# An mLSTM cell followed by a gated feed-forward block: three loads and one join of the first cells at other places in their queues

## The chip, the core and the metric

The kernel runs on one core of a Trainium2 chip. A core has a matrix engine (TensorE, PE in the profile, with its weight loads shown apart as PEld), a vector engine (VectorE, DVE), a scalar engine for activation functions (ScalarE, ACT), a general engine (GpSimd, POOL), and a queue processor (SyncE, SP) that here issues nearly all DMA transfers. Each engine takes its own instructions strictly in the order in which the program lists them, and they wait for one another through semaphores. The metric is the time of one execution on the device in microseconds (us), lower being better.

## The reference

The first half is a recurrent attention cell over 4 batches, 8 heads, 768 steps and a head width of 40; the second half multiplies its 3072 x 320 result by w_in (320 x 2048), applies h cos(h) and multiplies by w_out (2048 x 320).

```python
for t in range(S):
    m_new = np.maximum(f_gate[:, :, t] + m, i_gate[:, :, t])
    f_stab = np.exp(f_gate[:, :, t] + m - m_new)
    i_stab = np.exp(i_gate[:, :, t] - m_new)
    m = m_new
    C = f_stab[..., None, None] * C + i_stab[..., None, None] * np.einsum('bhd,bhe->bhde', vt, kt)
    n = f_stab[..., None] * n + i_stab[..., None] * kt
    h_tilde = np.einsum('bhde,bhe->bhd', C, qt)
    denom = np.maximum(np.abs(np.einsum('bhd,bhd->bh', n, qt)), 1.0)[..., None]
    y[:, :, t] = h_tilde / denom / (1.0 + np.exp(-o_gate[:, :, t]))
...
h = x @ w_in
return (h * np.cos(h)) @ w_out
```

## The kernel before

The recurrence is worked in chunks of 128 steps: 6 chunks c times 4 batches b make 24 cells, numbered n = 4c + b. In a cell, the scores q k^T of all 8 heads (`scores`, L440) are weighted by a decay matrix E and multiplied by v (`values`, L466); the state left by earlier chunks is added for n of 4 and more (`values_kept`). The result is normalized on VectorE (`normalize`), transposed on TensorE (`seam`) and copied by ScalarE into x^T (`seam_out`, L594), the input of the feed-forward block. That block works on one chunk of 512 tokens at a time. `Up` (L607) computes two 128-row blocks of h for a chunk: for each block one matmul with the first 128 rows of w_in, one with the second 128 (L621) and one with the last 64, held apart in `w_in_l` (L624). The profile shows every matmul of 32-bit floats as two instructions, so that an `Up` has four L621, four L621 again and four L624 there. `near`, `rest`, `sin` and `gate` turn h into h cos(h) on ScalarE and VectorE by turns; `down` multiplies by w_out (L754 in the first chunk, L697 later).

The program orders everything by hand. `first_cells` (L768) lists what happens for cells 0 to 3, before any feed-forward work; after it, `both_parts` (L904) runs one cell of chunk c + 1 beside two `Up`s of chunk c. Every call in `first_cells` adds its instructions to the ends of the queues of the engines it uses, so moving a call moves its instructions against all others on those engines, and on no other engine.

The steps that the change touches:

- `load(n, which)` (L315) issues the transfers of q, k and v of cell n on SP, 160 KB each, in rows of 40 numbers (L329). q, k and v have four buffers each, so cell 4 uses those of cell 0.
- `load_E(n)` (L340) issues, on SP, the broadcast of M, the running maximum of the gates, to all 128 partitions: 512 KB (L345). It lands in the tile E of the cell.
- `load_o` (L300) fetches o_gate, 160 KB a batch; `weights_in(f)` (L156) issues ten transfers that make three pieces of w_in: two with 128 rows each (four transfers each) and the last 64 rows (two transfers); `weights_out(p)` (L167) issues one of 640 KB. All these are on SP.
- The weights come as 64-bit floats, and are joined into 32-bit ones: `parts` (L132) works on ScalarE (L138, L140), and `join` (L143) runs three operations on VectorE (L144, L146, L148) and an addition (L149), on GpSimd unless VectorE is named.
- `decay_exponents(n)` (L370) subtracts a column from E on VectorE (L372) and masks it on GpSimd (L373); `decay(n)` takes Exp on ScalarE (L381). `weigh(n)` (L450) multiplies E by the scores (L453).

Up(0,0), the first feed-forward work, is special: between its first and second four matmuls it calls `cell_after_first` (L879):

```python
turn(B)                      # q and k of cell 4 transposed on TensorE
turn_out(B, False)           # copied by ScalarE
first_out = out_parts()      # w_out's first piece, L138 and L140 on ScalarE
decay(B)                     # Exp of cell 4 on ScalarE
weigh_k(B)
out_join(*first_out)         # w_out's first piece, L144 to L148 on VectorE
```

(B is 4.) After it, TensorE has the second four L621, the four L624 that use w_in_l, scores(4), values_kept(4), six warming matmuls and values(4).

Of the kernel before, what the change touches and what calls it, by code (L numbers as in the profile page):

```python
# [29 lines left out]
def kernel(  # L30
# [22 lines left out]
    B, H, S, D = q.shape  # L53
# [78 lines left out]
    def parts(dst, bits):  # L132
        n = dst.shape[1]
        hi, lo = bits[:, 0:n, 1], bits[:, 0:n, 0].bitcast(U32)
        t = p2.tile([128, WQ], I32, name="wt", tag="wt")[:, 0:n]
        m = p2.tile([128, WQ], I32, name="wm", tag="wm")[:, 0:n]

        nc.scalar.activation(out=t.bitcast(FP), in_=hi.bitcast(FP), func=AF.Abs)  # L138

        nc.scalar.activation(out=m, in_=lo, func=AF.Copy, scale=2.0 ** -29)  # L140
        return dst, hi, t, m

    def join(dst, hi, t, m, last=None):  # L143
        nc.vector.tensor_scalar(out=t.bitcast(FP), in0=t.bitcast(FP), scalar1=LEAST, scalar2=GREATEST,  # L144
                                op0=OP.max, op1=OP.min)
        nc.vector.tensor_scalar(out=t, in0=t, scalar1=5, scalar2=2, op0=OP.logical_shift_left,  # L146
                                op1=OP.logical_shift_right)
        nc.vector.scalar_tensor_tensor(out=t, in0=hi, scalar=TOP2, in1=t, op0=OP.bitwise_and, op1=OP.bitwise_or)  # L148
        (last or nc.gpsimd).tensor_tensor(out=dst.bitcast(I32), in0=t, in1=m, op=OP.add)  # L149
# [17 lines left out]
    def weights_out(p):  # L167
        bits = pc.tile([128, 2, DM, 2], I32, name="bits", tag="bits")
        src = w_out_bits.rearrange("(g e a r) n two -> g a r e n two", e=2, a=2, r=128)
        nc.sync.dma_start(out=bits, in_=src[p // 2, p % 2])  # L170
        return w_out_sb[:, ts(p, 2)].rearrange("p f n -> p (f n)"), bits.rearrange("p e n two -> p (e n) two")
# [29 lines left out]
    def later_fills():  # L201
        for i in range(1, NB):
            fill(i)
        for t in st:
            nc.gpsimd.memset(t, 0.0)
        for t in qbs:
            nc.gpsimd.memset(t[:, H * 64:], 0.0)
# [3 lines left out]
    def gates_in():  # L211
        nc.sync.dma_start(out=F0, in_=fg[:, 0:C])
        nc.scalar.dma_start(out=a0, in_=ig[:, 0:C])

    def later_gates_in():
        nc.sync.dma_start(out=F1.rearrange("r c s -> r (c s)"), in_=fg[:, C:])
        nc.sync.dma_start(out=a1.rearrange("r c s -> r (c s)"), in_=ig[:, C:])
# [74 lines left out]
    def load_o(c, bs=range(B)):  # L292
        if c not in sig:
            sig[c] = p2.tile([128, B * DM + LO], FP, name="o", tag="o")
            if c > 1:
                nc.gpsimd.memset(sig[c][:, B * DM:], 0.0)
        for b in bs:
            o = sig[c][:, ts(b, DM)]
            if c * B < TURNED:
                nc.sync.dma_start(out=o.rearrange("t (h d) -> t h d", h=H),  # L300
                                  in_=o_gate[b, :, ts(c, C)].rearrange("h t d -> t h d"))
                continue

            for k4 in range(HP):
                nc.sync.dma_start(out=o[ts(k4, 32)].rearrange("r (i x) -> r i x", i=2),
                                  in_=o_gate[b, ts(k4, 2), ts(c, C)].rearrange("i (r x) d -> r i (x d)", x=T4))
# [5 lines left out]
    def blocks(n):  # L312
        return [qbs[n % 2 + i].rearrange("r (p x) -> r p x", p=HP) for i in (0, 2)]

    def load(n, which="qkv"):  # L315
        c, b = divmod(n, B)
        i = n % NB
        if n >= TURNED:
            for dst, src in zip(blocks(n), (q, k)):
                src = src[b, :, ts(c, C)].rearrange("(p j) (r x) d -> j r p (x d)", j=2, x=T4)  # L320
                for j in range(2):
                    r = slice(64 * j, 64 * j + 32)
                    nc.sync.dma_start(out=dst[r], in_=src[j])
                    r = slice(64 * j + 32, 64 * j + 64)
                    nc.sync.dma_start(out=dst[r, :, 0:(T4 - 1) * D + DL], in_=src[j, :, :, DA:])
            which = "kv"
        for name, dst, src in (("q", qs[i], q), ("k", ks[i], k), ("v", vs[i], v)):
            if name in which:
                nc.sync.dma_start(out=dst[:, :, 0:D], in_=src[b, :, ts(c, C)].rearrange("h t d -> t h d"))  # L329
# [10 lines left out]
    def load_E(n):  # L340
        c, b = divmod(n, B)
        E = p4.tile([128, H, C], FP, name="E", tag="E")
        if n not in SPREAD:
            src = M_d[0][ts(b, H)] if c == 0 else M_d[1][ts(b, H), ts(c - 1, C)]
            nc.sync.dma_start(out=E, in_=src.unsqueeze(0).to_broadcast([128, H, C]))  # L345
        Es[n] = E
# [18 lines left out]
    def cols(n, j, width):  # L365
        c, b = divmod(n, B)
        return tab[:, c, j, ts(b, H)].unsqueeze(2).to_broadcast([128, H, width])


    def decay_exponents(n):  # L370
        E = Es[n]
        nc.vector.tensor_tensor(out=E, in0=E, in1=cols(n, 0, C), op=OP.subtract)  # L372
        nc.gpsimd.affine_select(out=E, in_=E, compare_op=OP.is_ge, fill=1.0e30, base=0,  # L373
                                pattern=[[0, H], [1, C]], channel_multiplier=-1)
# [388 lines left out]
    def warm(k, bank=None):  # L763

        for _ in range(k):
            nc.tensor.matmul(bank or pw, nil, nil.unsqueeze(1).to_broadcast([128, HP, 128]), start=True, stop=True)

    def first_cells():  # L768
        nc.vector.memset(nil, 0.0)
        gates_in()  # L770
        nc.scalar.copy(out=ident_b, in_=ident)
        load(0, "qk")
        later_gates_in()
        load(1, "qk")
        load(0, "v")
        load_o(0, (0, 1))
        load(2, "qk")
        load_E(0)
        load_E(1)
        warm(9)  # L780
        gates_first()
        later_fills()
        gates_first_out()
        wall_in(0, 0, pmu)
        wall_in(0, 1, psum_o())
        spread(0, 0)
        decay_exponents_half(0, 0)
        turn(0)
        turn_out(0, False)
        gates_sums()  # L790
        spread(0, 1)
        decay_exponents_half(0, 1)
        decay(0)
        weigh_k(0)
        load_E(2)
        load(1, "v")
        load(3, "qk")
        load_o(0, (2, 3))
        load_E(3)
        load(2, "v")  # L800
        load(3, "v")
        pieces.extend(weights_in(0))
        wall_in(1, 0, psum_o())
        wall_in(1, 1, psum_o())
        gates_less_sums()
        spread(1, 0)
        decay_exponents_half(1, 0)
        scores(0)
        gates_maxima()
        turn(1)  # L810
        weigh(0)
        turn_out(1, False)
        sigmoid(0, slice(0, 2))
        spread(1, 1)
        decay_exponents_half(1, 1)
        gates_exponents()
        decay(1)
        weigh_k(1)
        values(0)
        normalize(0)  # L820
        scores(1)
        turn(2)
        turn_out(2, False)
        warm(2)
        seam(0)
        weigh(1)
        seam_out(0)
        state(0)
        load(B)
        decay_exponents(2)  # L830
        decay(2)
        weigh_k(2)
        gates_exp()
        values(1)
        load_E(B)
        outs.append((0, weights_out(0)))
        load_o(1, (0,))
        load_E(B + 1)
        normalize(1)
        scores(2)  # L840
        turn(3)
        sigmoid(0, slice(2, 4))
        seam(1)
        weigh(2)
        decay_exponents(3)
        turn_out(3)
        gates_diagonal()
        seam_out(1)
        values(2)
        decay(3)  # L850
        weigh_k(3)
        state(1)
        normalize(2)
        scores(3)
        pg = gates_turn()
        warm(1)
        seam(2)
        weigh(3)
        join(*parts(*pieces.pop(0)))
        pieces.extend(weights_in(1))  # L860
        load(B + 1)
        outs.extend((p, weights_out(p)) for p in range(1, 3))
        load_o(1, (1, 2, 3))
        seam_out(2)
        second = parts(*pieces.pop(0))
        state(2)
        gates_keep(*pg)
        values(3)
        normalize(3)
        warm(5)  # L870
        seam(3)
        join(*second, nc.vector)
        decay_exponents(B)
        seam_out(3)
        join(*parts(*pieces.pop(0)), nc.vector)
        load_E(B + 2)
        state(3)

# [180 lines left out]
```

## Time and profile before

| | us |
|---|---|
| median of three runs | 540.45 |
| the three runs | 536.65, 540.67, 540.45 |
| the profiled execution's own time | 537.82 |
| its span in the profile | 536.1 |

The granted TensorE clock of the profiled execution is 1.0 throughout. The profile has the busy time of each engine, the waits with what released them, the chain of waits that ended last, and the order of instructions in time. Of the engine names, SPq, ACTq and DVEq mean the queue of an engine, in which it issues a transfer or passes a semaphore. A transfer's row on SPq is the time that issuing it took in the queue, what it waited for included; it lands later. Busy time of TensorE in a few stretches, from the view by windows:

| stretch, us | PE busy | DVE busy | ACT busy | DMA share | GB/s |
|---|---|---|---|---|---|
| 0 to 10 | 8.88 | 5.41 | 4.10 | 0.99 | 129 |
| 10 to 20 | 9.84 | 8.26 | 7.37 | 1.12 | 186 |
| 20 to 30 | 8.24 | 8.58 | 9.67 | 0.84 | 218 |
| 30 to 40 | 8.04 | 6.32 | 5.46 | 0.97 | 221 |
| 40 to 50 | 7.64 | 9.27 | 8.43 | 1.10 | 211 |
| 50 to 60 | 9.68 | 7.13 | 8.30 | 1.02 | 293 |
| 60 to 70 | 10.00 | 7.34 | 7.41 | 1.07 | 205 |

`first_cells` ends at about 35 us, where up(0,0) begins (L621 at 35.26).

### The profile page before, as it was taken

To read this page: it belongs to the slowest core of one execution; us is meant where nothing else is said; L and a number is where in the kernel's file an instruction comes from. 1 tells how busy PE (TensorE), PEld (TensorE's weight loads), DVE (VectorE), ACT (ScalarE), POOL (GpSimd) and SP (SyncE) were. 2 spreads that over 40 slices of the span, in tenths; PEclk is the share of its full clock that TensorE was granted. 3 is DMA by queue.
4 is the path that set the end of the run, shared out by engine and by line. 5 is a ranking of instruction groups with operands and counts; after the bars stand their busy time and mean duration, and the time that the engine had idled before them with its cause. 6 is when DMAs were issued, how large, how long until landed. Compare 5 with 4: busy or idle time off the path is not lost.

```text
span 536.1 us, 9942 instructions
## 1 busy us (share of the span) xinstructions
PE 524.8 (98%) x3634; PEld 332.6 (62%) x3634; DVE 365.7 (68%) x727; ACT 261.6 (49%) x416; POOL 168.0 (31%) x304
## 2 busy tenths in 40 slices
PE   9888999999999999999999999999999999999997
PEld 6755666665565666666666656656656756656555
DVE  6778778868677677777767777767776765422323
ACT  4868696765633445543436525427335322332312
POOL 7512433516253453223322322422212221212121
PEclk9999999999999999999999999999999999999999
DMA  9989995952265752166743076635075000010001
GB/s 139 214 214 250 230 225 164 196 113 46 73 139 125 165 109 62 51 140 144 159 99 82 14 174 134 141 82 123 6 177 107 14 15 11 6 49 0 2 0 49
DMA packets 134513, 56.86 MB, mean 106 GB/s; under 512 B 72081, under 2 KB 130529, under 8 KB 134465
## 3 DMA queue, kind: packets, MB, share of 16 engines
q1 hardware_dynamic: 134320, 56.04, 47.1%
q8 instruction: 28, 0.46, 0.4%
q0 software_dynamic: 96, 0.18, 0.2%
q14 instruction: 21, 0.16, 0.1%
q10 hardware_dynamic: 48, 0.02, 0.0%
HBM read 50.00 MB, written 6.21 MB: 105 GB/s over the span
## 4 chain that ended last, share of the span: by engine, by line
PE 80%; SPq 6%; DMA 5%; DVE 4%; ACT 4%; issue 1%; POOL 1%; DVEq 0%; ACTq 0%; POOLq 0%
PE po L697 32%; PE pup L621 28%; PE pup L624 9%; PE hp L490 3%; PE ps L447 3%; PE po L754 3%; DMA E<-M_d 2%; SPq L329 2%; PE hp L484 2%; SPq L129 1%; PE pu L586 1%; DMA bits<-in_moe_w_in_dram 1%; SPq L300 1%; DMA qs<-in_q_dram 1%; DVE n L632 1%
## 5 line engine op out<-in xcount | busy, mean ns | idle before, releaser
L621 PE MATMUL pup<-xT,w_in_sb 128*128 128x512 f32 x384 | 175.0, 598 | 0.7 <-DVE g L641 0.3
L629 ACT ACTIVATE n<-pup 128x512 int32<-128x512 f32 x96 | 52.0, 593 | 211.7 <-PE pup L624 211.7
L632 DVE SCALAR_TENSOR_TENSOR n<-pup,n 128x512 f32<-128x512 f32 x96 | 61.9, 686 | 122.1 <-ACT n L629 122.1
L697 PE MATMUL po<-w_out_sb,g 128*128 128x320 f32 (+1 forms) x480 | 118.6, 396 | 0.0
L621 PEld LDWEIGHTS pup<-xT,w_in_sb 128*128 128x128 f32 x384 | 69.7, 190 | 72.8 <-issue 63.4
L697 PEld LDWEIGHTS po<-w_out_sb,g 128*128 128x128 f32 x480 | 83.5, 190 | 36.7 <-issue 9.1
L680 POOL TENSOR_TENSOR sg<-g 128x128 f32<-128x128 f32 x80 | 36.7, 458 | 192.4 <-DVE g L641 191.0
L637 ACT ACTIVATE n<-n 128x512 f32<-128x512 f32 x96 | 58.9, 630 | 12.1 <-DVE n L632 12.1
L641 DVE SCALAR_TENSOR_TENSOR g<-pup,n 128x512 f32<-128x512 f32 x96 | 61.7, 685 | 2.5 <-ACT n L637 1.2
L624 PE MATMUL pup<-xT,w_in_l 64*128 64x512 f32 x192 | 54.2, 641 | 2.2 <-DVE w_in_l L149 2.2
L373 POOL TENSOR_SCALAR_AFFINE_SELECT E<-E 128x1024 f32<-128x1024 f32 x19 | 20.8, 1093 | 102.0 <-DVE E L372 81.0
L697 PE MATMUL po<-T,sg 128*128 128x160 f32 x240 | 39.4, 300 | 0.0
L624 PEld LDWEIGHTS pup<-xT,w_in_l 64*128 64x128 f32 x192 | 14.4, 184 | 38.7 <-issue 35.6
L754 PE MATMUL po<-w_out_sb,g 128*128 128x320 f32 x128 | 36.6, 439 | 0.1
L697 PEld LDWEIGHTS po<-T,sg 128*128 128x128 f32 x240 | 34.8, 190 | 0.2
L412 DVE STREAM_TRANSPOSE t<-qs 128x512 f32<-128x512 f32 x32 | 32.7, 1101 | 0.0
L447 PEld LDWEIGHTS ps<-t,t 40*128 40x128 f32 (+1 forms) x384 | 25.1, 188 | 9.7 <-issue 9.4
L453 DVE TENSOR_TENSOR E<-ps,E 128x512 f32<-128x512 f32 x48 | 30.7, 681 | 0.4 <-PE ps L447 0.4
L381 ACT ACTIVATE E<-E 128x1024 f32<-128x1024 f32 x21 | 22.2, 1057 | 17.4 <-POOL E L373 16.2
L754 PEld LDWEIGHTS po<-w_out_sb,g 128*128 128x128 f32 x128 | 23.7, 190 | 9.7 <-POOL w_out_sb L149 0.3
L447 PE MATMUL ps<-t,t 40*128 40x128 f32 (+1 forms) x384 | 25.8, 274 | 0.0
L372 DVE TENSOR_TENSOR E<-E,tab 128x1024 f32<-128x1024 f32 x19 | 23.1, 1216 | 3.3 <-DMA E<-M_d 3.3
(152 smaller groups left out, 640.6 us busy)
## 6 DMA issues: line engine op xcount, KB each, us to landing
E<-M_d SPq DMA_DIRECT2D x22, 512.0 KB
bits<-in_moe_w_in_dram SPq DMA_DIRECT2D x40, 128.0 KB
bits<-in_moe_w_out_dram SPq DMA_DIRECT2D x8, 640.0 KB
room<-G_d SPq DMA_DIRECT2D x32, 128.0 KB
ks<-in_k_dram SPq DMA_DIRECT2D x24, 160.0 KB
vs<-in_v_dram SPq DMA_DIRECT2D x24, 160.0 KB
qs<-in_q_dram SPq DMA_DIRECT2D x32, 80.0 KB
qs<-in_k_dram SPq DMA_DIRECT2D x32, 80.0 KB
```

The lines of the kernel that those rows point to most:

```text
L412: nc.vector.transpose(out=dst.rearrange("r p (t x) -> r p x t", x=T4), in_=src.rearrange("r p (x d) -> r p x d", x=T4)[:, :, :, 0:32])
L447: nc.tensor.matmul(ps[j][:, p], kT[r, p], qT[r, p], start=True, stop=True)
L453: nc.vector.tensor_tensor(out=w, in0=pss[n][j], in1=w, op=OP.mult)
L621: nc.tensor.matmul(pu, w_in_sb[:, i, ts(block(f2, e), 128)], x(i), start=(i == 0), stop=False)
L624: nc.tensor.matmul(pu, w_in_l[r, f2], x(NK, r), start=False, stop=True)
L629: nc.scalar.activation(out=self.n[e], in_=self.pu[e], func=AF.Copy, bias=0.25)
L632: nc.vector.scalar_tensor_tensor(out=self.n[e].bitcast(FP), in0=self.pu[e], scalar=0.25, in1=self.n[e], op0=OP.add, op1=OP.subtract)
L637: nc.scalar.activation(out=r, in_=r, func=AF.Sin, scale=TWO_PI_DOWN)
L641: nc.vector.scalar_tensor_tensor(out=g, in0=self.pu[e], scalar=TWO_PI, in1=self.n[e].bitcast(FP), op0=OP.mult, op1=OP.mult)
L680: nc.gpsimd.tensor_tensor(out=S[:, i], in0=x, in1=y, op=op)
L697: nc.tensor.matmul(out, g, w, start=(f2 == 0 and first), stop=end, skip_group_check=True)
L754: nc.tensor.matmul(po[c][b], gs[c, f][:, ts(b, C)], w_out_sb[:, f], start=(f == 0), stop=(f == NF - 1))
```

## The change

Five lines of `first_cells` move; no operation is added or taken away.

```diff
         load(3, "qk")
+        load(2, "v")
         load_o(0, (2, 3))
         load_E(3)
-        load(2, "v")
         load(3, "v")
         pieces.extend(weights_in(0))
...
         state(0)
-        load(B)
+        load_E(B)
+        load(B, "qk")
         decay_exponents(2)
...
         values(1)
-        load_E(B)
         outs.append((0, weights_out(0)))
+        load(B, "v")
         load_o(1, (0,))
...
         join(*second, nc.vector)
-        decay_exponents(B)
         seam_out(3)
         join(*parts(*pieces.pop(0)), nc.vector)
+        decay_exponents(B)
         load_E(B + 2)
```

On SP, v of cell 2 goes ahead of two loads of o_gate and of M of cell 3. M of cell 4 goes ahead of q, k and v of cell 4, and v of cell 4 goes behind w_out's first piece; the order there was q, k, v, M, w_out and is M, q, k, w_out, v. On VectorE, the four operations of the join of w_in's last 64 rows (L144, L146, L148 and L149, all on VectorE here) stand ahead of L372 of cell 4 instead of behind it. The order on TensorE, ScalarE and GpSimd is the same in both programs.

## The prediction, made before the changed kernel was run

> **What bounds the kernel now.** I read the page's busy table first, then who waited for whom on TensorE before and after 48 us, then the chain of waits between 26 and 49 us, then the order of time on each engine there.
>
> ```profile
> span 536.1 us, 9942 instructions
> PE 524.8 (98%) x3634; PEld 332.6 (62%) x3634; DVE 365.7 (68%) x727; ACT 261.6 (49%) x416; POOL 168.0 (31%) x304
> ```
>
> TensorE is busy 98% of the span, so only its holes can be won. From 48 us on, the view of waits for TensorE holds two entries, 0.5 us together. Before 48 us it holds these four among six:
>
> ```profile
> PE pup L624 <- DVE w_in_l L149: 2.2, 1, 2.2
> PE ph L472 <- DMA vs<-in_v_dram: 1.8, 1, 1.8
> PE pw L766 <- ACT st L600: 1.5, 1, 1.5
> PE pup L621 <- ACT xT L594: 0.2, 1, 0.2
> ```
>
> The change aims at the first (w_in's last rows, joined late on VectorE) and the second (v of cell 2). The chain of waits tells which of them carries the end (columns: start, us, what):
>
> ```profile
> 26.37 4.80 DMA bits<-in_moe_w_in_dram
> ...
> 31.27 0.67 ACT wt L138
> ...
> 32.26 5.68 DMA E<-M_d
> ...
> 38.03 1.23 DVE E L372
> ...
> 39.49 1.08 DVE wt L146
> ...
> 41.57 0.44 DVE w_in_l L149
> ...
> 42.05 1.13 PE pup L624 x4
> ...
> 44.17 1.29 DVE E L453 x2
> ```
>
> VectorE stands 2.52 us for M of cell 4 (E), subtracts, and only then joins w_in_l, for which TensorE stands 2.24 us. The v wait at 24.32 is not in it. The order of time on three engines gives the rows that I use (start, us, engine):
>
> ```profile
> 37.92 1.88 PE L621 MATMUL pup<-xT,w_in_sb 128*128 128x512 f32 x4
> 39.49 1.07 DVE L146 TENSOR_SCALAR wt<-wt 128x256 int32<-128x256 int32 x1
> 39.78 0.79 ACT L138 ACTIVATE wt<-bits 128x640 f32<-128x640 f32 x1 [1.02 <-DMA bits<-in_moe_w_out_dram]
> 41.13 1.04 ACT L381 ACTIVATE E<-E 128x1024 f32<-128x1024 f32 x1
> ```
>
> **The join ahead of the exponents.** VectorE is free at 35.50 (34.81 + 0.69), and ScalarE's two halves of that piece end at 35.76. The four operations without company cost 0.29 + 0.29 + 0.43 + 0.43 us (the same shapes at 39.17, 60.85, 61.18 and 41.57), with gaps 1.6 us: w_in_l is done at about 37.2 instead of 42.00. TensorE's second four L621 end at 39.80, so L624 starts there, not at 42.05: 2.25 us. Scores(4) start 0.96 us after it, and weigh(4) 1.16 us after those (43.01 and 44.17 now): 40.76 and 41.92.
>
> In place of that wait, three things could be late. First E4: its subtraction now starts after 37.2. M of cell 4 is issued where q of cell 4 was (28.36, with 1.40 us in the queue), and 5.68 us (now 32.26 to 37.94) puts it at 34.0 to 35.4, so the subtraction (1.23) ends at 38.4 and GpSimd's mask (1.09) at 39.6. Second, w_out's first piece stands on ScalarE ahead of cell 4's Exp: it lands at 39.7 now, 6.6 us after its issue at 33.17. It is issued one place earlier, and at M's old 32.26 would land at 38.9; if it were held until M has landed (the third issue after M of cell 2 lasted until 15.58, and that after M of cell 3 until 23.08) at 35.4, it lands at 40.4 by the 5.0 us of v2 (19.16 to about 24.2). Exp ends 2.39 us after the piece starts (39.78 to 42.17): 41.4 or 42.8. I take 41.4, since q and k, the issues between, took the queue 0.52 to 1.59 us each now. Third, VectorE's part of the w_out join, 1.88 us (41.91 to 43.79): from 39.8 to 41.7.
>
> So weigh(4) starts at 41.92, and the sine of up(0,0) waits for the longer of two ways. By VectorE it stays 1.92 us behind weigh (44.17, 46.09): 43.84. By ScalarE, after Exp come L629 (1.08) and a table load (1.28): 43.8 with Exp's end at 41.4, 45.2 with 42.8. Gain 2.25 us, or 0.85; I take 2.2.
>
> A row on company: L146 took 1.07 us at 39.49 beside GpSimd's mask of E (39.33 to 40.42), and 0.29 us at 60.85 without it. After the change the mask ends at 39.6 and the w_out join starts at 39.8; if they meet, 0.78 us falls there, of which 0.56 reaches weigh (41.7 against 41.92). [...]
>
> **Does it last to the end?** ScalarE has no gap from 46.09 to 58.3; it feeds L629 of up(0,1) at 55.13, VectorE's joins, and through GpSimd's L149 (58.71 to 59.98) the matmul at 60.00. All of that moves with the sine, provided nothing waits for a transfer: M of cell 5 was issued by 36.83 and lands by 42.5 (5.68 more), wanted at 44.4; w_in's next pieces were issued by about 44.8 and are wanted from 46.8 to 55.4, the first of them issued before 42.9. From 60 us TensorE is packed and the others wait for it (ScalarE 2.27 us before L629 at 64.76), so the shift stays.
>
> **v of cell 2 earlier.** It goes out at 15.62 instead of 19.16 and lands near 20.7; values(2) then starts when weigh(2) and TensorE allow (22.6, not 24.32). These 1.7 us I cost at nothing: normalize(2) waits behind E3's subtraction, kT and the diagonal on VectorE (which end at 25.9 now), and weigh(3) at 27.94 waits for Exp of cell 3 (26.85 to 27.91), at the end of a ScalarE queue full since 20.18. Behind it, seam(3) waits for warm(5), which waits for L600 on ScalarE, held behind w_in's second piece (landed 31.17). What v2 is moved past is late by 160 KB at 222 GB/s, 0.74 us: the two o_gate loads (wanted at 22.51 by the sigmoid) and M of cell 3 (landed near 23.3, wanted at once). Its subtraction starting at 24.05 pushes weigh(3) by 0.3 to 0.7, but seam(3) has 0.9 (normalize(3) ends at 33.14, the seam starts at 34.10). The w_in pieces have the same bytes ahead of them as before. Bounds 0.9 faster (all the slack of the seam, if w_in came earlier too) and 0.74 slower; I take 0.2 slower, nearer to a bytes count that is unchanged. [...]
>
> **q, k, v of cell 4 later.** v (wanted after 43) is covered. The turn of q and k stands on TensorE between the two halves of up(0,0), at 37.05 and 37.48. k is issued in v's old place (30.49 to 32.08) and by 5.0 us lands at 35.5 to 37.1. No cost taken.
>
> Sum: 2.2 - 0.2 = 2.0 us off the profiled execution's 537.82 us (span 536.1 and 1.7 around it): 535.8. The median shown is 540.45, 2.6 above that execution; from it the sum gives 538.45. The runs lie 4 us apart, so I name the middle of both, 537.1.
>
> **Rivals.** (1) The gain is given back on ScalarE: the w_out piece lands at 40.4 or later, Exp ends at 42.8, and the sine moves by 0.85, with v2's loss by 0.1 to 0.8. For it: the held third issues after M. Against it: fewer issues ahead. Time near 538.5 by the same middle. (2) v2 pays too: w_in's second piece lands earlier and seam(3) moves up by its 0.9: 3.1 in all, 536.0. Against it: the unchanged bytes. (3) Slower: k of cell 4 stops TensorE in the middle of up(0,0). If k's issue is held until M of cell 4 has landed (34.0 to 35.4), 5.0 us more is 39.0 to 40.4; the transposes follow, then four L621 (1.88) and L624. Now L624 starts 4.57 us after the k transposes (37.48 to 42.05), and needs 2.32 after them (37.48 to 39.80), so k decides from 39.7 on: L624 would start at 42.7, 0.7 later than now, with v2's 0.74 up to 1.4 slower, 540.1. Against it: k is second after M, and the second issue after M of cells 2 and 3 went out in 0.69 and 0.58 us.
>
> **How the numbers follow.** Forecast (1.2 to 2.5 faster) 0.62, rival 1 0.2, rival 2 0.08, rival 3 0.1. The range takes the lower run 536.65 less 2.3, 534.3, to the upper runs with no gain left, 540.5; the runs' own spread fills most of it. About 1%, 5.4 us, is the least that a measurement can tell from no change, and no case reaches it: 0.9 within, 0.06 faster (a base that fell high and a full gain), 0.04 slower.
>
> **What would show it.** Right: no wait of L624 for w_in_l, L624 near 39.8, sine near 43.9, the L621 of up(0,2) near 57.8; no wait for v at values(2), yet weigh(3) still near 28 and up(0,0) still starting near 35.3. Wrong: a wait of the turn for k, ScalarE waiting for w_out past 40, a first L621 after 36, or a new wait for a transfer between 44 and 60.

## The result, and the profile after

| | before, us | after, us |
|---|---|---|
| median (14 runs each) | 539.35 | 538.85 |
| lowest and highest run | 536.65, 541.19 | 536.74, 540.88 |
| ratio of the times, with its 95% interval | | 0.9991 [0.9971, 1.0011] |
| the profiled execution's own time | 537.82 | 540.05 |
| its span | 536.1 | 538.3 |
| its mean granted TensorE clock | 1.0 | 0.987 |

The change makes no difference that can be measured. The time lies in the range given, 534.3 to 540.5, and the base was about right (the middle of the two bases was 539.1, the median of 14 runs is 539.35), but the gain of 2.0 us did not come: the medians differ by 0.5 us, within the interval. The profiled execution of the changed kernel is even 2.2 us longer than that of before. The page says where to look (first two rows: span and busy times; third: granted clock in 40 slices of 13.5 us, in tenths).

```profile
span 538.3 us, 9940 instructions
...
PE 530.4 (99%) x3634; PEld 336.6 (63%) x3634; DVE 364.6 (68%) x727; ACT 261.3 (49%) x416; POOL 168.4 (31%) x304
...
PEclk9959999999999999999999999999999999999999
```

TensorE has the same 3634 matmuls as before and is busy 5.6 us longer (530.4 against 524.8). The third slice, 26.9 to 40.4 us, has a granted clock of 0.5, where before had 9s throughout: this execution ran the work just ahead of up(0,0) at half clock. The waits of TensorE before 48 us, where the two waits that the change aims at stood:

```profile
PE ps L447 <- DVE t L436: 2.3, 1, 2.3
PE pw L766 <- DVE nil L769: 1.1, 1, 1.1
...
```

(The two entries left out are of 0.2 us.) The 2.2 us for w_in_l and the 1.8 us for v are gone, and so are the 1.5 us for L600. At their head stands a new stop of 2.3 us: scores(3) (ps, L447) waits for a copy on VectorE (t, L436). The chain of waits shows what held that copy, and that from there to the feed-forward block the time is TensorE's own (start, us, what):

```profile
19.20 6.17 DMA E<-M_d
...
25.39 0.04 DVE E L372
...
26.53 0.69 DVE t L436
...
27.36 2.08 PE ps L447 x16
...
33.22 3.57 PE ph L472 x16
...
40.13 1.96 PE pup L621 x4
```

M of cell 3 (E), which now has v of cell 2 ahead of it as well as the two o_gate loads, lands at 25.36 instead of near 23.3; VectorE subtracts (L372) and only then copies. And the rows on TensorE are long: the 16 matmuls of values(3) take 3.57 us in the chain, where one L472 group of before took 1.98. The view by windows fixes when that was so (columns: us, busy time and instructions of PE, PEld, DVE, ACT, POOL, then granted clock, DMA share, GB/s):

```profile
24.00:25.00 1.00, 1.00 (x10) 0.94 (x9) 0.00 (x0) 0.99 (x2) 0.00 (x0) 1.00 1.11 269
25.00:26.00 1.00, 0.06 (x1) 0.00 (x0) 0.61 (x1) 0.98 (x3) 0.00 (x0) 0.80 1.04 238
26.00:27.00 1.00, 0.00 (x0) 0.00 (x0) 1.00 (x2) 0.98 (x2) 0.31 (x1) 0.50 1.04 256
...
39.00:40.00 1.00, 0.91 (x19) 0.54 (x17) 0.93 (x2) 0.49 (x2) 0.00 (x0) 0.87 1.25 214
```

The clock halves at about 25.6 (a mean of 0.80 in that microsecond is 0.4 us at half) and is whole again at about 39.25: 13.65 us. In this execution up(0,0) starts at 40.13, where the prediction had 35.3. Behind it, the stop that the change was to remove is absent, as the order of time on TensorE shows, first before:

```profile
35.26 1.95 PE L621 MATMUL pup<-xT,w_in_sb 128*128 128x512 f32 x4 [0.22 <-ACT xT L594]
...
48.44 3.70 PE L621 MATMUL pup<-xT,w_in_sb 128*128 128x512 f32 x8 [0.32 <-DVE g L641]
```

and after:

```profile
40.13 1.96 PE L621 MATMUL pup<-xT,w_in_sb 128*128 128x512 f32 x4 [0.22 <-ACT xT L594]
...
44.61 1.13 PE L624 MATMUL pup<-xT,w_in_l 64*128 64x512 f32 x4
...
51.01 2.41 PE L621 MATMUL pup<-xT,w_in_sb 128*128 128x512 f32 x5 [0.32 <-DVE g L641]
```

L624 follows without a stop, and from up(0,0) to up(0,1) it is 51.01 - 40.13 = 10.88 us, against 48.44 - 35.26 = 13.18 before: 2.30 us less, near the forecast 2.2. These rows alone do not say whether the join's new place removed the stop, or whether TensorE came so late that the join would have been done in its old place too. So the questions are why the work ahead came 4.9 us later, whether the change did that, and what an execution of the kernel before looks like when it comes as late.

### The profile page after: what moved, and what is told of

Same layout as the page of the kernel before. It is cut to its first block, busy times and chain, and to the rows that moved or that the text cites. A ratio compares the mean times of both kernels' runs of the same rounds, so it can differ in the third digit from the quotient of the medians.

```text
span 538.3 us, 9940 instructions
## 1 busy us (share of the span) xinstructions
PE 530.4 (99%) x3634; PEld 336.6 (63%) x3634; DVE 364.6 (68%) x727; ACT 261.3 (49%) x416; POOL 168.4 (31%) x304
## 4 chain that ended last, share of the span: by engine, by line
PE 90%; SPq 3%; ACT 2%; DVE 1%; DMA 1%; issue 1%; POOL 0%; POOLq 0%; ACTq 0%
PE po L697 32%; PE pup L621 30%; PE pup L624 9%; PE po L754 6%; PE ps L447 4%; PE hp L490 3%; SPq L329 2%; PE hp L484 2%; PE ph L472 2%; PE pu L586 1%; DMA E<-M_d 1%; SPq L300 1%; PE pw L766 0%; PE pq L462 0%; PE pt L428 0%
## 5 line engine op out<-in xcount | busy, mean ns | idle before, releaser
L621 PE MATMUL pup<-xT,w_in_sb 128*128 128x512 f32 x384 | 175.0, 598 | 0.7 <-DVE g L641 0.3
L621 PEld LDWEIGHTS pup<-xT,w_in_sb 128*128 128x128 f32 x384 | 69.7, 190 | 72.8 <-issue 63.2
L624 PE MATMUL pup<-xT,w_in_l 64*128 64x512 f32 x192 | 54.2, 641 | 0.0
L373 POOL TENSOR_SCALAR_AFFINE_SELECT E<-E 128x1024 f32<-128x1024 f32 x19 | 20.7, 1091 | 105.9 <-DVE E L372 81.4
L697 PE MATMUL po<-T,sg 128*128 128x160 f32 x240 | 39.4, 300 | 0.0
L624 PEld LDWEIGHTS pup<-xT,w_in_l 64*128 64x128 f32 x192 | 14.4, 184 | 36.4 <-issue 36.4
L447 PEld LDWEIGHTS ps<-t,t 40*128 40x128 f32 (+1 forms) x384 | 25.9, 193 | 12.0 <-issue 11.6
L453 DVE TENSOR_TENSOR E<-ps,E 128x512 f32<-128x512 f32 x48 | 30.7, 681 | 0.1
L447 PE MATMUL ps<-t,t 40*128 40x128 f32 (+1 forms) x384 | 26.8, 280 | 2.3 <-DVE t L436 2.3
L372 DVE TENSOR_TENSOR E<-E,tab 128x1024 f32<-128x1024 f32 x19 | 23.1, 1216 | 2.2 <-DMA E<-M_d 2.2
```

The costliest lines, as they stand in the source:

```text
L447: nc.tensor.matmul(ps[j][:, p], kT[r, p], qT[r, p], start=True, stop=True)
L453: nc.vector.tensor_tensor(out=w, in0=pss[n][j], in1=w, op=OP.mult)
L621: nc.tensor.matmul(pu, w_in_sb[:, i, ts(block(f2, e), 128)], x(i), start=(i == 0), stop=False)
L624: nc.tensor.matmul(pu, w_in_l[r, f2], x(NK, r), start=False, stop=True)
L697: nc.tensor.matmul(out, g, w, start=(f2 == 0 and first), stop=end, skip_group_check=True)
```

## The experiments

Every execution leaves its mean granted clock. In the profiles the half clock (0.50) lasts 3.40 us (mean clock 0.996), 6.82 (0.994), about 10.4 (0.990, from windows of 10 us), 13.65 (0.987) or 17.06 (0.984), each worked out from the view by windows: near one to five stretches of 3.41 us, of which each takes 3.41 / 2 over 536, or 0.0032, from the mean. So the clocks of many executions give an estimate of how often and how long a kernel is slowed, without a profile of each. The ratios below are to the kernel before, on the same chip.

**Which part brings the half clock?** One theory: v of cell 2, by making M of cell 3 late, opens the new stop and with it brings the drop. The rival: the drop comes in the kernel before too, and the one profiled execution happened not to have it. Four kernels: the one before against itself, the join alone, v of cell 2 alone, and the change without v of cell 2.

The kernel before:

> The kernel before itself, to see the span and granted clock of every one of its executions. Theory A (the change pays in the join and loses it in a clock dip that v of cell 2 brings): nearly all executions have a mean clock of 0.997 or more, spans 535 to 537. Rival B (the dips come with or without the change, at chance times): clocks scatter from 0.987 to 1.0 as they do after the change (0.987 to 0.997), with spans of 535 to 539, and the scatter of the times comes from them.

It measured 0.9978 [0.9953, 1.0003] against itself, with clocks from 0.984 to 0.997; so a ratio of 0.998 is here what no change at all can give. The rival is right: of the 136 executions of the kernel before whose clock is known, 61 have 0.990 or less, with a mean span of 538.9 us, and 71 have 0.994 or more, with 536.3. These two groups make much of the scatter of its runs, not all of it: within the upper group the spans still go from 534.8 to 538.6. The profiled execution of before, at 1.0, was of the upper kind, and a rare one: only 7 of the 136 have 1.0.

The join alone, and v of cell 2 alone:

```diff
-        decay_exponents(B)
         seam_out(3)
         join(*parts(*pieces.pop(0)), nc.vector)
+        decay_exponents(B)
```

> Only the join of w_in's last rows ahead of cell 4's exponents; all loads as before. Theory A: M of cell 4 still lands near 37.9, so the subtraction starts no earlier than before, Exp of cell 4 ends near 42.2, and the sine of up(0,0) moves by about 1.5: ratio 0.997 at equal clocks, clocks as before. Rival B: the same gain, clocks scattered as after the change.

```diff
+        load(2, "v")
         load_o(0, (2, 3))
         load_E(3)
-        load(2, "v")
```

> Only v of cell 2 ahead of o_gate and M of cell 3. Theory A: M of cell 3 lands 1 to 2 later, TensorE stands 2 or more between values(2) and scores(3), the clock drops to 0.5 there, mean clock 0.987 to 0.997, 1 to 4 slower than before (ratio 1.002 to 1.007). Rival B: clocks as before, ratio 0.999 to 1.002.

Join alone 0.9984 [0.9960, 1.0009], v alone 0.9980 [0.9958, 1.0003]; clocks of 0.990 or less in 5 of 12 executions of each, as often as before. In their executions of 0.994 or more the mean spans are 536.4 and 536.5, against 536.3 before. Neither part alone is worth anything that shows.

The change without v of cell 2, that is M of cell 4 first in the queue and the join:

```diff
-        load(2, "v")
         load_o(0, (2, 3))
         load_E(3)
+        load(2, "v")
```

(This edit is against the changed kernel.)

> The change without its first part: M of cell 4 first and the join first, v of cell 2 where it was. Theory A: the 2.2 of the join arrive, clocks as in the kernel before, ratio 0.996 (0.994 to 0.998). Rival B: clocks as after the change, ratio 0.998 to 1.001.

0.9982 [0.9956, 1.0008]. Seven executions with a clock of 0.994 or more have a mean span of 535.4, 0.9 below the kernel before over all sessions; three with 0.987 have 538.2, where the kernel before has 538.4. That looks like a gain where the clock holds, but it is not shown here: the seven executions of this kind of the kernel before itself, in the run above, have 535.7.

**Is there a gain when the clock is made to hold, and none when it never holds?** Warming matmuls (128 x 512 in bf16, results unused, as the kernel has them elsewhere) were added around the small matmuls of values(0) and values(2), to before and to after, and in another pair three of the existing ones were taken out.

```diff
+        warm(3, psum_o())
         values(0)
...
+        bank = psum_o()
+        warm(4, bank)
         values(2)
+        warm(4, bank)
```

> The kernel before with 3 warming matmuls ahead of values(0) and 4 on either side of values(2) (2.4 us of extra TensorE work at 0.216 each, much of it in holes). Theory (clock and join do not add: the join's wait of 2.2 exists only where the clock held at 1.0, and where it dropped TensorE comes to L624 so late that w_in_l has long been there): the clock now holds in nearly all executions (0.997 or more), spans 535 to 537, median below the kernel before by 1.5 to 3. Rival (the dips do not depend on how densely TensorE works there): clocks scatter as before, and the extra matmuls cost 0 to 2.

> The changed kernel with the same warming matmuls. Theory: clock held, and the join's gain shows whole: 1.5 to 2.3 below the kernel before with the warming matmuls, spans 533.5 to 535, L624 near 40 without a wait. Rival: within 0.7 of it, at any clock.

The clock held at 0.994 or more in all 24 executions. Still, before with warming measured 0.9983 [0.9961, 1.0004] and after with warming 1.0003 [0.9978, 1.0027]. In before with warming, L624 still stops for the join; in after with warming it does not. Rows of TensorE from each, first before with warming:

```profile
41.71 1.13 PE L624 MATMUL pup<-xT,w_in_l 64*128 64x512 f32 x4 [1.21 <-DVE w_in_l L149]
...
83.82 0.63 PE L428 MATMUL pt<-ident,ks 128*128 128x128 f32 x4 [1.01 <-PE pt L428]
```

and after with warming:

```profile
40.43 1.13 PE L624 MATMUL pup<-xT,w_in_l 64*128 64x512 f32 x4
...
84.35 0.64 PE L428 MATMUL pt<-ident,ks 128*128 128x128 f32 x4 [1.99 <-issue]
85.11 5.22 PE L621 MATMUL pup<-xT,w_in_sb 128*128 128x512 f32 x8
```

L624 starts 1.28 us earlier in the second, and up(0,1) at 47.37 instead of 48.10, 0.73 earlier. But at the turn of cell 7 (its q and k transposed on TensorE, L428) there is a stop in both, 1.01 and 1.99 us, and the L621 behind it start at 84.59 and 85.11: the lead is gone, and in the second the clock halves after the stop (eight L621 in 5.22 us instead of 3.67). The stop itself ends with the transposes of k, for which the view names no transfer or engine that released them; the L621 behind them start as a join ends, and the chain of waits of after with warming leads from that join back to a transfer:

```profile
71.52 1.06 DMA bits<-in_moe_w_in_dram
...
83.83 1.28 POOL w_in_sb L149
```

ScalarE began at 72.69 (L138) on a piece of w_in that landed at 72.58, and the chain goes on through what it does behind it, down to GpSimd's part of the next piece's join, 83.83 to 85.11, which came last; in before with warming the same join ends at 84.59. So what these two executions gained ahead of 60 us was lost to the transfers. An earlier start of the feed-forward block does not by itself explain the stop: the kernel before had its L621 at 83.42 without one, with its up(0,1) at 48.44. In these two the queue was later: it had issued the last of these w_in transfers by 72.4 and 72.1, in the kernel before by 70.0. Why is not shown.

The pair without three existing warming matmuls:

```diff
-        warm(2)
         seam(0)
...
-        warm(1)
         seam(2)
```

> The kernel before without the warming matmuls ahead of seam(0) and seam(2) (three in all). Theory: the clock drops in nearly all executions, mean 0.984 to 0.99, spans 537.5 to 540, and L624 does not wait for w_in_l. Rival: clocks as in the kernel before.

> The changed kernel without those three warming matmuls. Theory: the clock drops in nearly all executions as well, and the time is that of the kernel before without them, within 0.7: the join has nothing to gain. Rival (the join's gain adds to the dip's cost): 1.5 to 2.3 below it.

Before so cooled: 1.0004 [0.9980, 1.0028], no clock above 0.994, but only five of twelve at 0.990 or less, where nearly all were expected; in its profile (0.984) L624 starts at 44.92 with no stop for the join, although the join is in its old place. After so cooled: 1.0000 [0.9980, 1.0020]; eight of twelve clocks at 0.990 or less, and one of 0.994. The two differ by nothing that can be measured: where TensorE is slowed, this stop leaves nothing to win.

**Do the later transfers hold the gain back?** The w_out pieces, 640 KB each, were issued one step later, and this was crossed with the change and with the warming.

```diff
-        outs.extend((p, weights_out(p)) for p in range(1, 3))
+        outs.extend((p, weights_out(p)) for p in range(1, 2))
...
-        if p + 3 < NF // 2:
-            outs.append((p + 3, weights_out(p + 3)))
+        if p + 2 < NF // 2:
+            outs.append((p + 2, weights_out(p + 2)))
```

> The kernel before with every piece of w_out after the second fetched one step later (a prefetch of two pieces instead of three), so that 640 KB less stand ahead of w_in's third part and of q and k of cell 7 in the queue. Theory (between 60 and 85 the transfers, not TensorE, set how early the work can be, so what TensorE gains before 60 is given back at the turn of cell 7): the kernel before has a wait for L624 at about 42 in any case, so it gains little: 0 to 0.7 at equal clocks. Rival (the floor is not the transfers): nothing, or a loss where a piece of w_out comes late.

> The changed kernel with the same fetch of w_out. Theory: in executions whose clock holds (0.996 or more) the gain of the join lasts: spans 534 to 535, 1 to 2 below the kernel before with the same fetch; where the clock drops to 0.99 or less, no difference. Rival: as the changed kernel, spans of 535.0 to 536.3 at held clocks.

> The kernel before with the warming matmuls around values(0) and values(2) and the later fetch of w_out. Theory: clock held in most executions, the stop at the turn of cell 7 (1.0 in the trace with the warming alone) gone: spans 535 to 536, narrower than 535.3 to 539.4. Rival: spans scattered as with the warming alone.

> The changed kernel with both. Theory: the stop at the turn of cell 7 (2.0 in the trace with the warming alone) is gone, the clock holds, and the gain of L624 (1.3 between the two warmed traces) lasts to the end: spans 533.7 to 535, 1.0 to 1.5 below the kernel before with both. Rival: within 0.5 of it.

| w_out one step later, with | ratio to before | clocks of 0.994 or more: mean span |
|---|---|---|
| before | 0.9998 [0.9971, 1.0024] | 2 of 12: 535.7 |
| after | 0.9964 [0.9937, 0.9990] | 6 of 12: 534.9 |
| before and warming | 0.9961 [0.9936, 0.9985] | 12 of 12: 536.0 |
| after and warming | 0.9933 [0.9911, 0.9955] | 10 of 10: 534.7 |

The last has the lowest median of this study: 536.40 us, where the kernel before had 540.30 beside it, and its slowest run, 537.41, is below the medians of before (540.30) and of before with the same warming and fetch (537.84). The later fetch alone gives nothing (0.9998); with the change but without warming the two are clear of no change (0.9964), though six of those twelve executions were slowed. The stop at the turn of cell 7 is gone (from the L621 at 72.39 to the next at 83.26 it is 10.87 us, against 13.63 in after with warming). With the clock held and that stop gone, the change is worth 536.0 - 534.7 = 1.3 us of mean span (standard error 0.36, from the spread of the executions), or 1.1 if only executions with a clock of 1.0 are compared (535.7 and 534.7).

The profile of before with w_out later shows the order of the kernel before, up to this point, with a drop (clock 0.984). By windows, around the wait for v:

```profile
23.00:24.00 1.00, 0.00 (x0) 0.00 (x0) 0.20 (x1) 0.99 (x1) 0.00 (x0) 1.00 1.20 223
24.00:25.00 1.00, 0.36 (x3) 0.39 (x3) 1.00 (x2) 0.97 (x2) 0.00 (x0) 0.87 0.66 169
25.00:26.00 1.00, 1.00 (x6) 1.00 (x7) 1.00 (x3) 0.98 (x3) 0.90 (x1) 0.50 0.83 242
```

and the same stretch of the kernel before's own profile:

```profile
23.00:24.00 1.00, 0.00 (x0) 0.00 (x0) 0.66 (x1) 0.99 (x2) 0.00 (x0) 1.00 1.29 244
24.00:25.00 1.00, 0.68 (x7) 0.71 (x7) 1.00 (x2) 0.98 (x2) 0.35 (x1) 1.00 1.00 280
25.00:26.00 1.00, 1.00 (x12) 1.00 (x11) 0.87 (x2) 0.98 (x3) 1.00 (x2) 1.00 0.62 164
```

The same instructions, nearly the same hole of TensorE (1.9 and 1.8 us in the waits): in the one the clock halves at about 24.7, in the other it stays. In the first, L624 starts 3.8 us later than in the second (45.85 against 42.05) and without a stop, with the join in its old place:

```profile
45.85 1.13 PE L624 MATMUL pup<-xT,w_in_l 64*128 64x512 f32 x4
```

**What remains.** Two more profiles of the changed kernel, to see it with the clock held, and two tests of what the kernel with the lowest median needs: without v of cell 2 earlier, and with six warming matmuls behind values(2) in place of four ahead of it and four behind.

> The changed kernel once more, one profile, to catch an execution whose clock held (4 of 14 did). Theory if the clock is 0.994 or more: L624 near 40 without a wait for w_in_l, and the 2 that it gains partly given back between 60 and 86, by a stop at the turn of cell 7 or a wait of ScalarE for w_in's third part. If the clock is lower: as the profile after, L624 near 44, no wait.

> The changed kernel for a second such profile. Theory: with a clock of 0.994 or more, L624 near 40 without a wait and a stop or late ScalarE between 60 and 86; with a lower one, L624 near 44. Rival: L624 near 42 even with the clock held.

The first came at a clock of 0.994 (two stretches at half clock, 15.7 to 22.5, early), 537.82 us; the second at 0.987, 540.53 us, with a stop of 2.8 us at scores(3), like the profile after. The first shows up(0,0) at 37.36 and up(0,1) at 48.77: 11.41 us, not 10.88. VectorE and GpSimd between them, in the order of time (a bracket holds the idle time before a row):

```profile
41.36 1.09 POOL L373 TENSOR_SCALAR_AFFINE_SELECT E<-E 128x1024 f32<-128x1024 f32 x1 [5.93 <-DVE E L372]
41.59 1.22 DVE L144 TENSOR_SCALAR wt<-wt 128x640 f32<-128x640 f32 x1 [0.30 <-ACT wt L138]
...
42.43 0.95 POOL L394 TENSOR_TENSOR kw<-ks,tab 128x320 f32<-128x320 f32 x1
...
42.80 1.06 PE L447 MATMUL ps<-t,t 64*128 64x128 f32 x16
42.83 0.89 DVE L146 TENSOR_SCALAR wt<-wt 128x640 int32<-128x640 int32 x1
...
44.50 1.28 DVE L453 TENSOR_TENSOR E<-ps,E 128x512 f32<-128x512 f32 x2
```

The w_out join meets GpSimd's mask of E (L373) and the kw of cell 4 (L394): L144 takes 1.22 us and L146 0.89, where each took 0.49 in the kernel before:

```profile
41.91 0.49 DVE L144 TENSOR_SCALAR wt<-wt 128x640 f32<-128x640 f32 x1
42.43 0.49 DVE L146 TENSOR_SCALAR wt<-wt 128x640 int32<-128x640 int32 x1
```

The weigh (L453) starts 1.70 us after scores(4), where the prediction had 1.16.

> The change without its first part (v of cell 2 stays behind M of cell 3), with the warming matmuls and the later fetch of w_out. Theory: clock held, L624 as early as with v moved, since the seam waits for w_in's second piece either way: within 0.5 of the changed kernel with both, spans 534 to 535.5. Rival (v's place matters once the clock holds): 1 or more away from it.

> The changed kernel with the later fetch of w_out and the warming matmuls only ahead of values(0) (3) and behind values(2) (6, in the stop that v's move made there), none ahead of values(2). Theory: the clock holds in most executions, spans 533.5 to 535 where it does. Rival: the 4 ahead of values(2) were needed too, and a third or more of the executions drop to 0.99 or less.

Without v of cell 2: 0.9949 [0.9923, 0.9974]; at a clock of 1.0 its mean span is 534.63, against 534.66 with v of cell 2 earlier (seven executions each). With the six behind values(2) and none ahead of it: 0.9952 [0.9932, 0.9972], clock 0.995 or more in all twelve. So in this kernel the place of v is worth nothing, and nine warming matmuls do about as well as eleven.

## Why the prediction was right or wrong

The traces of this study put the disputed stretch side by side (us; up(0,1) is the next L621 of an `Up`):

| execution | clock | up(0,0) starts | stop before L624 | L624 to up(0,1) |
|---|---|---|---|---|
| before | 1.0 | 35.26 | 2.24 | 6.39 |
| before again | 0.996 | 36.00 | 1.57 | 6.39 |
| before, warming | 1.0 | 35.95 | 1.21 | 6.39 |
| before, warming, w_out later | 1.0 | 35.92 | 0.61 | 6.39 |
| before, cooled | 0.984 | 39.56 | none | 6.39 |
| before, w_out later | 0.984 | 40.94 | none | 6.39 |
| after | 0.987 | 40.13 | none | 6.40 |
| after, second profile | 0.994 | 37.36 | none | 6.93 |
| after, warming | 1.0 to 84 us | 35.95 | none | 6.94 |
| after, warming, w_out later | 1.0 to 47 us | 35.92 | none | 6.92 |

**Right.** The join ahead of the exponents takes 1.6 us (40.72 to 42.36 in the profile after, 38.51 to 40.16 in its second profile) and no trace with the join ahead has a stop before L624; in the traces whose clock held, where the kernel before has one, this is the join's doing. v of cell 2 earlier removes the wait of values(2) and is worth nothing; M of cell 4 first does not make k late (no stop at the turn in the middle of up(0,0)), nor is w_out's piece late on ScalarE (L138 of 640 starts at 43.52 and at 40.75, without a wait). k did stand in the queue for 2.48 us in the profile after, longer than the 0.6 to 0.7 set against the third rival, and still came in time. So the rivals fell: ScalarE gives nothing back, v does not pay, k stops nothing.

**Wrong: "up(0,0) still starting near 35.3", and the 2.25 us taken from it.** The step read the stop off one execution and took TensorE's arrival for fixed. L624 of the kernel before is tied to M of cell 4 and the join behind it, at 41 to 42 us; how long TensorE stops there depends on when TensorE comes. When it comes follows how long the clock was halved: over all traces up(0,0) starts at 35.3 to 36.1 with at most one stretch ahead of it, at 37.4 with two, at 38.7 and 38.9 with three, and at 39.4 to 40.9 with four or five, whichever of the loads and the join were moved. From 39.4 on the stop is nothing, in the kernel before's order too; 61 of 136 executions of before and 9 of 14 of after have a clock of 0.990 or less. The profiled execution was the earliest arrival seen, so its 2.24 us was the largest stop seen. At a clock of 0.986 or 0.987 the spans are 538.4 before (33 executions) and 538.6 after (3); at 0.994 or more 536.3 before (71) and 536.0 after (4). At equal clocks little or nothing of the 2.25 is left.

**Wrong: the meeting of the w_out join and GpSimd's mask, "if they meet", left at nothing.** With the clock held they do meet: L624 to up(0,1) is 0.54 longer than before (6.93 against 6.39). The size given, 0.56, came out near by luck: VectorE lost 1.13 us (0.73 and 0.40 on the two operations) where 0.78 was given, and had 0.59 us of room where 0.22 was given. The choice to leave it out was the error. In the slowed execution they do not meet at that price (6.40). In the pair with warming and w_out later, the profiled executions have 47.47 and 47.32 for up(0,1): of the 0.68 us that L624 is earlier, 0.53 are given back here. These two profiles differ by 0.15 us only, and of the two the changed kernel's has the longer span (535.6 and 534.8). So the 1.1 to 1.3 us of mean span are not seen in a trace. They may lie in executions where before stops longer (its spans at a clock of 1.0 go from 534.8 to 536.8, those of after from 533.9 to 535.2). A late M of cell 4 in those would do it; no trace shows one, and this is left open.

**Wrong: "What v2 is moved past is late", bounded at 0.74 us by its bytes.** M of cell 3 was put at 24.05 at the latest and landed at 25.36, and TensorE stopped 2.3 us for what follows it on VectorE, a stop that the prediction did not have: the hole that v left ahead of values(2) opened again behind it. It is no chance of one execution: where VectorE stands for this transfer, its L372 starts at 22.73 (before, cooled) and 23.34 (before) with v in its old place, and at 25.06 (after, with warming, and with w_out later too), 25.26 (after, cooled) and 25.39 (after) with v earlier. In the pair with warming, too, VectorE waits 0.81 us for it at 25.06 with v earlier, while in before with warming it has landed by 24.16. In the kernels with warming it cost no time in the end, as the spans with and without v show (534.66 and 534.63).

**"Does it last to the end?"** A lateness does: the profile after is 2.6 us behind that of before at up(0,1) and 2.2 at the end. A lead need not: with the warming matmuls it met a limit that the step did not look for, a piece of w_in that landed at 72.6 us and the joins behind it.

What the 0.5 us between the medians is made of, if it is more than chance, is not shown. The slowed executions of the changed kernel (0.990 or less) have a mean span of 537.7 against 538.9, because six of the nine have three stretches where the kernel before mostly has four or five; but they are more frequent, 9 of 14 against 61 of 136. The numbers are too small to tell whether the change does either.

**Not settled:** whether the change makes the clock drop more often (of kernels without added warming, 29 of 52 executions with v earlier and 85 of 184 with v in its old place have 0.990 or less), and what exactly decides in one execution that the clock drops. That more work on TensorE around values(0) and values(2) keeps it is shown (68 of 68 executions at 0.994 or more, in six kernels with warming), and with less work it held less often (3 and 1 of 12 there in the cooled pair, 71 of 136 in the kernel before). Why two executions with nearly the same hole differ is not.

## What to carry to other kernels

Before a stop of TensorE is priced, look at the granted clock of several executions: a stop that ends with a transfer or a join at a fixed time is only as long as TensorE is early, and the profile that has the earliest TensorE shows the longest stop (here 2.24 us with up(0,0) at 35.26, none at 39.56 and 40.94 with the join in the same place). Where executions scatter in steps of the clock, make the clock hold first (a few warming matmuls in the stretches of small ones: 0.994 or more in 68 of 68 executions here), then look for the next transfer that the earlier work runs into, and only then move a join: the three together gave 0.9933 [0.9911, 0.9955], the first two without the change 0.9961 [0.9936, 0.9985], the change or its join by itself nothing that could be told from no change. An instruction moved on VectorE is to be drawn against GpSimd's at its new time (L144 took 1.22 us beside GpSimd's mask here, 0.49 without), and the price of their meeting is counted unless a row shows that they miss each other.

## What the runs showed of the hardware

Where the granted clock drops, the rows have it at 0.50 for a time near a whole number of stretches of 3.41 us: 13.65 us in the profile after is four of them, the other traces have 3.40, 6.82, about 10.4 and 17.06, and 104 of the 136 executions of the kernel before have a mean clock of 1.0, 0.997, 0.994, 0.990, 0.987 or 0.984, the values for none to five. The drop of the profile after came 0.5 us after TensorE's last matmul (values(2) ended at 25.06, the clock fell at about 25.6), in a stop of 2.3 us in all, and with TensorE shown busy for the whole 3 us ahead of it (2.00 of 2.00 us from 22 to 24, and 1.00 of 24 to 25), with small matmuls (128 x 41 in 32-bit floats, 23.08 to 25.06) and transposes. Which of these brings the drop is not shown.

The drop lasts differently long with the place of v of cell 2, though no ratio shows a gain. Of kernels without added warming, those with v earlier have a clock of 0.989 or 0.990 (three stretches) in 15 of 52 executions and 0.984 (five) in 1; those with v in its old place have them in 4 and 35 of 184. No run explains this.

VectorE beside GpSimd: VectorE's L144 on 640 columns took 1.22 us beside GpSimd's mask and its L146 0.89 beside kw in the second profile of the changed kernel, against 0.49 each in the kernel before, where GpSimd was idle; GpSimd's mask kept its 1.09 us. The mask had 0.86 us left when L144 began (41.59 to 42.45), and L144 took 0.73 longer than alone; in the profile after it had 0.27 left (44.38 to 44.65), and L144 took 0.13 longer (0.62). What makes VectorE slower beside it is not shown.
